# The opening of a transformer block: order of loads, normalisation and first projections

## Chip, cores and metric

One core of a Trainium2 chip. The metric is the device time of one execution in microseconds (us), median of several runs.

## What is computed

One pre-norm block over 2048 tokens of width 576: attention with 32 query heads of 18 columns that share one key and one value head, then a bilinear feed-forward part of width 4608.

```
S, D, H, Dh, F = 2048, 576, 32, 18, 4608
n  = layernorm(x)
q  = n @ wq          (32 heads);   k = n @ wk;   v = n @ wv      (one head each)
o  = softmax(q k^T * Dh**-0.5) v
h  = x + o @ wo
n2 = layernorm(h)
out = h + ((n2 @ w_gate) * (n2 @ w_up)) @ w_down
```

The layer norm has no weights. The order of the tokens inside the softmax's sum doesn't matter, and each token's output depends on its own row and on all keys and values, so tokens may be permuted inside the kernel if the output is put back in the same order.

## The kernel before

Tokens are worked in four blocks of 512 (`TB`), each as four tiles of 128 rows. The kernel gives each engine its program by hand (`manual_schedule`): the order of the Python calls is the order on each engine and on SP, which issues all DMAs. Matrices that need full precision are split into a high part (a cast to `fp32r`) and a low part (the rest, a subtraction), and a product is three matmul passes: high by high, high by low, low by high. A projection of one block is 14 such passes over 512 columns (`passes`, line 1187).

`keys_values` (line 131) is the opening. SP loads the tokens tile by tile, block 0, then the constants, the weights of keys and values (`wkr`) and of the first seven query heads (`wqr0`), then blocks 1 to 3, and last the other three query weights. Then:

- `stats` (line 166) takes mean and variance of a tile on VectorE; `scale` (171) takes the inverse root by Newton steps on VectorE (block 0) or POOL, with -mean x rstd always on POOL; `apply` (179) normalises a tile on ScalarE;
- `turn` (185) transposes a block on TensorE, 16 transposes into two large PSUM tiles `tr` and 8 for the last 128 rows into `trt`; `parts` (201) splits the result into the block's `XT`, the cast on ScalarE, the subtraction on VectorE (`split`, line 82; `split_tail`, line 91);
- `project` (212) makes queries of the last four heads, keys and values of one block (`psk`); `mean` and `keys` (217, 222) take the mean key of block 0 away and store the keys, in three parts, into `kT` by DMA; `values` (249) transposes values into `V`;
- `weights` (256) splits a query weight; `query` (262) makes 7 heads' queries of block 0, one matmul a step; `ready` (268) splits them, and `store_q` (363) takes their absolute values (`tq`) and stores the queries to memory;
- `bound` and `bounds` (240, 410) work out an upper bound of each query's scores (`psb`, `psg`), which `load_m` brings beside the queries from `load_q` (454, 460) as two more rows; with it the exponential needs no maximum.

`pair` (513) is one step of attention: two score matmuls over 128 keys and two heads each (`s`, two PSUM tiles of two banks in turn), and one exponential of 1024 columns on ScalarE (`P`, line 534). Two pairs and the `acc` matmuls (line 538) of earlier pairs are a `step`. The opening issues 14 pairs between its projections. A block and a group of four heads have 32 pairs, a block 256.

The main loop follows (line 1129): two pairs, then 1.9 units (`RATE`) of the generator `queries` for all blocks (380), which makes the queries of blocks 1 to 3, one unit being two half matmuls (line 389). For block 0 it only stores the last four heads, waits 7 units and makes the last bounds. Then `blocks` (1056) goes on with pairs up to the 256th (`steps`, line 994), beside output projections (`yo`, line 689) of block 0, and the feed-forward part, in which the attention of later blocks is mixed.

A tile of 128 tokens is 128 consecutive rows, one to a partition (lines 145, 877, 983).

Of the kernel before, what the change touches and what calls it, by code (L numbers as in the profile page):

```python
# [25 lines left out]
P = 128  # L26
# [28 lines left out]
class Block:  # L55
# [9 lines left out]

    def ps_s(self, name):
        return self.ps.tile([P, 2, TB], F32, tag="s", bufs=2, name=name)
# [34 lines left out]
    def rstd(self, var, name, eng=None, n=NQ):  # L102
# [6 lines left out]
        dve.tensor_scalar(v, var, 1e-5, None, ALU.add)  # L109
# [21 lines left out]
    def keys_values(self):  # L131
# [39 lines left out]
        def scale(lo, hi, eng):  # L171
            r = self.rstd(mv[:, lo:hi, 1], f"a{lo}", eng, hi - lo)
            n = self.lp.tile([P, hi - lo], F32, tag=f"n{hi - lo}", name=f"n{lo}")
            pool.tensor_tensor(n, mv[:, lo:hi, 0], r, ALU.mult)
            pool.tensor_scalar(n, n, -1.0, None, ALU.mult)
# [3 lines left out]
        def apply(b, lo=0, hi=NQ):  # L179
            for s in range(lo, hi):  # L180
                xh = xhs[s] = self.pp.tile([P, D], F32, tag="P", name=f"xh{b}_{s}") if b < 2 else xs[b][:, s, :]
                r, n = rs[NQ * b + s]
                act.activation(xh, xs[b][:, s, :], AF.Identity, bias=n, scale=r)

        def turn(b):

            tail = self.ps_m(f"trt{b}")
            for r in range(2):
                tr = self.ps_s(f"tr{b}_{r}").rearrange("p a (c q) -> p (a c) q", q=2 * P)
                for s in (2 * r, 2 * r + 1):  # L190
                    for c in range(4):
                        pe.transpose(tr[:, c, (s - 2 * r) * P:(s - 2 * r + 1) * P],
                                     xhs[s][:, c * P:(c + 1) * P], self.ident)
                trs.append((b, r, tr))
# [6 lines left out]
        def parts():  # L201

            while trs:
# [8 lines left out]
        def project(b):  # L212
            psk = psks[b] = (self.ps_a if b < 2 else self.ps_f)(f"psk{b}")
            for i, (w, m) in enumerate(passes(w_h, w_l, self.XT[b])):
                pe.matmul(psk[:6 * DH], w, m, start=(i == 0), stop=(i == 13))

# [32 lines left out]
        def values(lo, hi):  # L249
            psv = (self.ps_m if lo else self.ps_a)(f"psv{lo}").rearrange("p (t c) -> p t c", c=64)  # L250
# [5 lines left out]
        def weights(i, cast):  # L256

            w, r = cols[i], wqr[i]
            cast(self.wq_h[w], r)
            pool.tensor_tensor(self.wq_l[w], r, f32(self.wq_h[w]), ALU.subtract)  # L260

        def query(i):
            psq = psqs[i] = self.ps_f(f"psq0_{i}")
            for k, (w, m) in enumerate(passes(self.wq_h[cols[i]], self.wq_l[cols[i]], self.XT[0])):
# [3 lines left out]
        def ready(i, copy):  # L268
# [4 lines left out]
            self.store_q(0, 7 * i, 7, qs, 0 if i else 4)  # L273
            yield
# [11 lines left out]
        q0, q1, q2, q3 = (query(i) for i in range(4))  # L286
        act.copy(w_h, wkr)
        stats(0, 4)
        scale(0, 4, dve)
        apply(0)  # L290
        pool.tensor_tensor(w_l, wkr, f32(w_h), ALU.subtract)
        weights(0, act.copy)
        stats(4, 8)
        scale(4, 8, pool)
        turn(0)
        parts()
        weights(1, act.copy)
        weights(2, pool.tensor_copy)
        stats(8, 12)
        scale(8, 12, pool)  # L300
        project(0)
        apply(1)
        some(q0, 4)
        turn(1)
        some(q0, 10)
# [790 lines left out]
    def run(self):  # L1096
# [8 lines left out]
        with ExitStack() as st:  # L1105
# [38 lines left out]
            self.guard()  # L1144


RATE = 1.9
P_BUFS = 6
QS = 3

# [128 lines left out]
```

## Time and profile before

| | us |
|---|---|
| median of 3 runs (2287.66 to 2289.48) | 2287.97 |
| the profiled execution | 2291.63 |
| its span, first to last instruction | 2289.8 |
| TensorE busy / ScalarE / VectorE / POOL | 2263.5 / 1443.3 / 1175.7 / 681.6 |
| mean granted TensorE clock | 0.997 |

The span is what the profile's times count from; the rest of the execution's time lies around it. A busy TensorE isn't one at its peak: a matmul at half the clock is busy twice as long. The chain of work that ended last is followed back from the last instruction through whatever released each step. A row of the timeline gives start, length, engine, line, operation and tiles, how many instructions are merged in it, and in brackets how long the engine was idle before and who ended that.

### The profile page before, as it was taken

Reading aid. Unit: us, or ns where it says so; the run is one execution under the profiler, and the core shown is the slowest. Engines: PE = TensorE matmul, PEld = TensorE weight load, DVE = VectorE, ACT = ScalarE, POOL = GpSimd, SP = SyncE. Lnnn points to the kernel's source line nnn. Section 1 sums busy time; section 2 is a strip of 40 time slices with the busy share of each in tenths; the row PEclk is TensorE's granted clock in tenths of the full one; section 3 lists DMA queues with packets and bytes.
Section 4 is the critical chain, followed back from the end, with each engine's and each line's share of the span. In section 5 each row is a group of like instructions: output and inputs, shape, how many; then the busy total and the mean of one; then the engine's idle time right before and its main releaser. Section 6 shows DMA issues by size and latency. Waiting matters only on the chain.

```text
span 2289.8 us, 45889 instructions
## 1 busy us (share of the span) xinstructions
PE 2263.5 (99%) x18090; PEld 1609.9 (70%) x18090; DVE 1175.7 (51%) x2134; ACT 1443.3 (63%) x1884; POOL 681.6 (30%) x862
## 2 busy tenths in 40 slices
PE   7999999999999999999999999999999999999998
PEld 5333345777777677677777777777777788888887
DVE  6332246565656576344444455444444476566665
ACT  5899977667676765767677767667677623232332
POOL 4000002545545454222222222222122233333342
PEclk9999999999999999999999999999999999999999
DMA  4212224433334443633333344634233355655553
GB/s 157 77 62 84 81 83 128 150 136 134 126 126 151 146 158 118 215 116 125 102 117 120 125 128 125 193 117 125 94 122 122 113 180 172 213 171 171 176 187 112
DMA packets 129434, 306.76 MB, mean 134 GB/s; under 512 B 17809, under 2 KB 17937, under 8 KB 129209
## 3 DMA queue, kind: packets, MB, share of 16 engines
q1 hardware_dynamic: 129209, 303.73, 40.7%
q8 instruction: 145, 2.38, 0.4%
q14 instruction: 80, 0.66, 0.1%
HBM read 233.76 MB, written 55.67 MB: 126 GB/s over the span
## 4 chain that ended last, share of the span: by engine, by line
PE 96%; ACT 1%; DVE 1%; issue 1%; DMA 1%; POOL 0%; SPq 0%; DVEq 0%; ACTq 0%; POOLq 0%
PE pg L925 21%; PE acc L538 20%; PE y L885 17%; PE gu L925 13%; PE s L533 12%; PE pu L925 5%; PE yo L689 3%; PE psq L389 2%; PE y L843 1%; ACT P L534 0%; PE psq L265 0%; DMA X<-X 0%; PE ye L843 0%; DVE XT L85 0%; PE tx L758 0%
## 5 line engine op out<-in xcount | busy, mean ns | idle before, releaser
L534 ACT ACTIVATE P<-s 128x1024 f32<-128x1024 f32 x1024 | 1024.9, 1026 | 271.1 <-PE s L533 195.0
L925 PE MATMUL pu<-X,ws 64*128 64x512 f32 x2592 | 702.2, 389 | 0.1
L925 PE MATMUL pg<-X,ws 64*128 64x512 f32 x2592 | 702.0, 389 | 0.0
L925 PEld LDWEIGHTS pg<-X,ws 64*128 64x128 f32 x2592 | 479.3, 185 | 67.8 <-issue 1.2
L538 PE MATMUL acc<-P,V 128*32 128x512 f32 x4096 | 488.8, 599 | 0.0
L925 PEld LDWEIGHTS pu<-X,ws 64*128 64x128 f32 x2592 | 477.1, 185 | 14.0 <-DVE h L690 1.0
L533 PE MATMUL s<-q,kT 56*128 56x512 f32 x2048 | 454.7, 422 | 4.4 <-ACT P L534 2.3
L885 PEld LDWEIGHTS y<-wdo,room 128*128 128x128 f32 x2856 | 386.0, 188 | 46.9 <-issue 44.2
L885 PE MATMUL y<-wdo,room 128*128 128x288 f32 x2856 | 402.8, 300 | 0.0
L892 ACT COPY tmp<-y 128x288 f32<-128x288 f32 x408 | 162.6, 399 | 330.1 <-PE y L885 311.3
L533 PEld LDWEIGHTS s<-q,kT 56*128 56x128 f32 x2048 | 210.7, 184 | 193.9 <-ACT P L534 116.0
L925 PE MATMUL gu<-X,ws 64*128 64x512 f32 x2592 | 301.6, 389 | 0.0
L893 POOL TENSOR_TENSOR x<-x,tmp 128x288 f32<-128x288 f32 x204 | 158.9, 809 | 434.4 <-ACT tmp L892 433.6
L538 PEld LDWEIGHTS acc<-P,V 128*32 128x32 f32 x4096 | 114.0, 109 | 243.1 <-issue 234.6
L925 PEld LDWEIGHTS gu<-X,ws 64*128 64x128 f32 x2592 | 249.7, 184 | 46.1 <-issue 4.6
L84 POOL CAST ws<-wr 128x1152 fp32r<-128x1152 f32 x144 | 171.7, 1193 | 322.4 <-PE pu L925 186.6
L893 POOL TENSOR_TENSOR h<-h,tmp 128x288 f32<-128x288 f32 x204 | 158.9, 806 | 344.8 <-ACT tmp L892 344.4
L85 DVE TENSOR_TENSOR ws<-wr,ws 128x1152 fp32r<-128x1152 f32 x144 | 198.6, 1379 | 74.6 <-POOL ws L84 74.6
L959 DVE TENSOR_TENSOR hf<-pu,g 128x512 f32<-128x512 f32 x96 | 66.4, 691 | 262.5 <-ACT g L955 259.1
L888 DVE TENSOR_TENSOR x<-x,y 128x288 f32<-128x288 f32 x272 | 117.2, 453 | 144.8 <-PE y L885 144.8
L888 DVE TENSOR_TENSOR h<-h,y 128x288 f32<-128x288 f32 x272 | 118.0, 454 | 111.9 <-PE y L885 109.0
L85 DVE TENSOR_TENSOR room<-S,room 128x1024 fp32r<-128x1024 f32 x68 | 86.3, 1270 | 146.5 <-ACT room L84 146.5
(170 smaller groups left out, 1628.2 us busy)
## 6 DMA issues: line engine op xcount, KB each, us to landing
wdo<-wd_dram SPq DMA_DIRECT2D x369, 288.0 KB
wr<-in_wgu_dram SPq DMA_DIRECT2D x144, 576.0 KB
wd_dram<-wdo SPq DMA_DIRECT2D x123, 288.0 KB
q<-q_dram SPq DMA_DIRECT2D x64, 216.0 KB
raw<-in_wd_dram SPq DMA_DIRECT2D x36, 288.0 KB
q_dram<-qs SPq DMA_DIRECT2D x15, 504.0 KB
X<-X SPq DMA_DIRECT2D x24, 256.0 KB
x<-in_x_dram SPq DMA_DIRECT2D x16, 288.0 KB
```

Source lines behind the costliest of these rows:

```text
L84: (copy or self.cast)(hi, src)
L85: self.dve.tensor_tensor(lo, src, f32(hi), ALU.subtract)
L533: self.pe.matmul(s_[:, i], self.kT[o:o + 56, t * P:(t + 1) * P], q[o:o + 56, pr], start=True, stop=True)
L534: self.act.activation(p_, s_, AF.Exp, scale=SCALE)
L538: self.pe.matmul(acc[32 * j:32 * j + 32, :], self.V[:, t, :], Ps[j // 2][:, j % 2, :], start=(t == 0), stop=(t == NT - 1), skip_group_chec ...
L689: pe.matmul(y[:, :HD], m, k, start=(i == 0), stop=(i == len(ms) - 1))
L885: pe.matmul(y[:, :HD], m[:, t * P:(t + 1) * P], k, start=(first and j == 0), stop=(j == 2), skip_group_check=True)
L888: dve.tensor_tensor(hs, hs, y[:, :HD], ALU.add)
L892: act.copy(z, y[:, :HD])
L893: pool.tensor_tensor(hs, hs, z, ALU.add)
L925: pe.matmul(ps, w[o:o + 64, wk, c], X[o:o + 64, xk, c], start=(j == 0), stop=(j == 26))
L959: dve.tensor_tensor(hf, pu, g, ALU.mult)
```

## The change

- **Tokens.** A block's 512 tokens lie four consecutive rows to a partition: tile s holds rows 4p + s. Loads of whole blocks are one DMA; block 0 comes in three (tile 0, tile 1, tiles 2 and 3). The stores of the output follow.
- **Order of loads.** Block 0, constants, key and value weights, two query weights, block 1, two query weights, blocks 2 and 3. The raw query weights 1 to 3 lie in buffers that the output weights use later, not in those of the queries.
- **Statistics and normalisation.** The inverse root has one operation less; on VectorE -mean x rstd is one VectorE operation and not two on POOL. `apply` takes a list of tiles, and an engine: VectorE normalises tiles 0 and 1 of blocks 0, 1 and 3 and all of block 2, ScalarE the others.
- **TensorE.** 24 transposes of the identity into a scratch bank come first (`WARM`). A projection of block 0's queries or of keys runs all passes of high parts first (`highs_first`). The query tiles q0 and q1 come ahead of block 1's transposes, q2 ahead of block 1's keys; the first score pairs follow those keys.
- **Query weights.** High parts of weights 0 to 2 on ScalarE, of 3 on POOL, each apart from its low part; 0 and 1 ahead of the normalisation.
- **Storing.** `store_q` is a generator: first stores, then `tq`, then the rest. Block 0's last four heads and all its bounds are done in the opening; the main loop starts at block 1.
- **Later.** `steps` always takes two units of output projection.

```diff
+    def tokens(self, dram, b):
+        return dram[b * TB:(b + 1) * TB, :].rearrange("(p s) d -> p s d", s=NQ)
...
-        dve.tensor_scalar(v, var, 1e-5, None, ALU.add)
+        dve.tensor_scalar(v, var, 1e-5, -0.5, ALU.add, ALU.mult)
         dve.tensor_copy(t, v.bitcast(I32))
-        dve.tensor_scalar(yi, t, -0.5, 1597463007.0, ALU.mult, ALU.add)
-        dve.tensor_scalar(v, v, -0.5, None, ALU.mult)
+        dve.tensor_scalar(yi, t, -0.5, 519526879.0, ALU.mult, ALU.add)
...
-        wqr += [self.qb.tile([P, 5, 7 * DH], F32, tag="qs", bufs=QS, name=f"wqr{i}") for i in range(1, 4)]
-        for b in range(NB):
-            for s in range(NQ):
-                sp.dma_start(xs[b][:, s, :], self.x[b * TB + s * P: b * TB + (s + 1) * P, :])
-            if b == 0:
-                sp.dma_start(self.C, self.cst)
-                sp.dma_start(wkr, self.wkv)
-                sp.dma_start(wqr[0], self.wq[cols[0]])
-        for w, r in zip(cols[1:], wqr[1:]):
-            sp.dma_start(r, self.wq[w])
+        wqr += [self.w0.tile([P, 5, 7 * DH], F32, tag="wo_r", bufs=3, name=f"wqr{i}") for i in range(1, 4)]
+        for lo, hi in ((0, 1), (1, 2), (2, 4)):
+            sp.dma_start(xs[0][:, lo:hi], self.tokens(self.x, 0)[:, lo:hi])
+        sp.dma_start(self.C, self.cst)
+        sp.dma_start(wkr, self.wkv)
+        for i in range(2):
+            sp.dma_start(wqr[i], self.wq[cols[i]])
+        sp.dma_start(xs[1], self.tokens(self.x, 1))
+        for i in range(2, 4):
+            sp.dma_start(wqr[i], self.wq[cols[i]])
+        for b in range(2, NB):
+            sp.dma_start(xs[b], self.tokens(self.x, b))
...
+            else:
+                dve.scalar_tensor_tensor(n, mv[:, lo:hi, 0], -1.0, r, ALU.mult, ALU.mult)
...
+                if on is dve:
+                    dve.tensor_scalar(xh, xs[b][:, s, :], mv[:, NQ * b + s, 0:1], r, ALU.subtract, ALU.mult)
+                else:
+                    act.activation(xh, xs[b][:, s, :], AF.Identity, bias=n, scale=r)
...
-            for i, (w, m) in enumerate(passes(w_h, w_l, self.XT[b])):
+            for i, (w, m) in enumerate(highs_first(w_h, w_l, self.XT[b])):
...
+        warm = self.ps_a("warm")
+        for _ in range(WARM):
+            pe.transpose(warm[:, 0:P], self.ident, self.ident)
+        stats(0, 4)
+        highs(0, act.copy)
+        highs(1, act.copy)
+        scale(0, 4, dve)
+        apply(0, 0, 1, on=dve)
+        apply(0, 2, 3)
         act.copy(w_h, wkr)
+        turns(0)
+        stats(4, 6)
+        parts()
         pool.tensor_tensor(w_l, wkr, f32(w_h), ALU.subtract)
+        lows(0)
+        lows(1)
+        highs(2, act.copy)
+        lows(2)
+        stats(6, 8)
         scale(4, 8, pool)
+        drain(project(0))
         mean()
+        some(q0, 15)
+        stats(8, 9)
         k0 = keys(0)
+        some(k0)
+        stats(9, 10)
         g0 = bound(G0, 1)
+        some(q1, 3)
         some(g0)
         t0 = ready(0, act.copy)
+        some(t0, 2)
         some(g0)
         some(t0)
+        some(k0)
+        some(q1, 6)
+        self.bounds(0, act.copy, self.pp.tile([H, 2, TB], F32R, tag="P", name="m2_0"), G0)
+        apply(1, 0, 1, on=dve)
+        apply(1, 2, 3)
+        stats(10, 11)
+        some(q1, 6)
         q = self.qt[0, 0] = self.qp.tile([P, 2, TB], F32R, tag="q", name="q0_0")
         some(k0)
         self.load_q(q, 0, 0)
         self.load_m(q, 0, 0)
+        some(t0)
+        t1 = ready(1, act.copy)
+        some(t1)
+        stats(11, 12)
+        scale(8, 12, pool)
+        highs(3, pool.tensor_copy)
+        lows(3)
+        values(0, 4)
+        turns(1)
+        parts()
+        stats(12, 14)
+        scale(12, 14, pool)
+        some(q2, 15)
+        drain(project(1))
+        apply(2, 0, 1, 2, 3, on=dve)
         k1 = keys(1)
         some(k1, 2)
+        self.pair()
+        self.pair()
+        stats(14, 15)
+        t2 = ready(2, act.copy)
+        some(t2)
+        some(q3, 6)
+        turns(2)
         parts()
         some(k1)
+        some(q3, 4)
+        stats(15, 16)
+        scale(14, 16, dve)
+        step(q3, 0)
+        values(4, 8)
+        drain(project(2))
+        apply(3, 0, 1, on=dve)
+        apply(3, 2, 3)
+        drain(t1)
+        drain(t2)
+        turns(3)
         k2 = keys(2)
         some(k2, 2)
         parts()
         some(k2)
+        some(q3, 15)
+        drain(ready(3, dve.tensor_copy))
+        self.last_heads(0)
         step()
         step()
+        drain(project(3))
         k3 = keys(3)
         some(k3, 3)
+        step()
+        step()
         g0 = bound(self.G, 4)
         some(g0, 2)
         values(8, 16)
+        self.pair()
+        self.bounds(0)
+        self.pair()
+        self.flush(len(self.pend) - 1)
...
-        if b in (0, NB - 1):
-            yield 4 if b else 7
+        if b == NB - 1:
+            yield 4
             self.bounds(b)
...
-            self.outs(2 if len(self.yos) > 1 else 1)
+            self.outs(2)
...
-                        for b in range(NB):
+                        for b in range(1, NB):
                             yield from self.queries(b)
...
+WARM = 24
+def highs_first(W, Wl, XT):
+    p = passes(W, Wl, XT)
+    return p[0:12:3] + p[2:12:3] + p[1:12:3] + p[12:]
```

In the part from `warm` to `flush` the added lines stand in their new order; lines without a mark stand in both kernels, and the old order is in the listing above.

More of the change, by code (lines that the diff above doesn't have):

```diff
@@ L199, in turn, with turns, parts @@
             trs.append((b, None, tail))
-        def parts():
-            while trs:
+        def turns(b):
+            for r in range(2):
+                turn(b, r)
+            turn_tail(b)
+        def parts(n=3):
+            for _ in range(n):
                 b, r, tr = trs.pop(0)
@@ L333, in keys_values @@
         parts()
         some(k1)
-        some(q1, 3)
-        values(0, 8)
-        some(ready(1, dve.tensor_copy))
-        step(q2, 4)
-        step(q2, 3)
-        apply(3)
-        project(2)
-        turn(3)
+        some(q3, 4)
[9 more added lines that the diff above has]
+        turns(3)
         k2 = keys(2)
@@ L981, in load_x @@
         h = self.h[b] = self.hp.tile([P, NQ, D], F32, tag="h", name=f"h{b}")
[L982 to L983 removed]
+        self.sp.dma_start(h, self.tokens(self.x, b))
     def fill(self, time, keep=2):
```

107 lines of the change are left out of this document (38 added, 69 removed).

## The prediction

> **What bounds the kernel now.** I read the page first: the shares by engine and the chain that ended last.
>
> ```profile
> PE 2263.5 (99%) x18090; PEld 1609.9 (70%) x18090; DVE 1175.7 (51%) x2134; ACT 1443.3 (63%) x1884; POOL 681.6 (30%) x862
> PE 96%; ACT 1%; DVE 1%; issue 1%; DMA 1%; POOL 0%; SPq 0%; DVEq 0%; ACTq 0%; POOLq 0%
> ```
>
> TensorE carries 96% of the chain, so an opening that ends earlier moves everything behind it. What such a change can win is TensorE time that is empty or slow. I cut the opening into windows to find it; after the window and its length the columns are busy us (and instructions) of each engine, granted clock, DMA share and GB/s.
>
> ```profile
> 12.50:18.00 5.50, 5.43 (x25) 5.08 (x25) 3.75 (x10) 4.81 (x8) 2.62 (x6) 1.00 1.06 382
> 40.00:42.00 2.00, 0.18 (x4) 0.09 (x2) 1.94 (x4) 0.15 (x1) 1.50 (x8) 0.94 0.44 127
> 42.00:52.00 10.00, 10.00 (x28) 4.71 (x29) 2.52 (x4) 6.59 (x8) 1.92 (x2) 0.50 0.27 88
> 52.00:76.50 24.50, 23.97 (x142) 13.62 (x142) 10.20 (x16) 15.11 (x18) 0.00 (x0) 1.00 0.17 51
> 83.90:298.80 214.90, 214.67 (x1566) 80.36 (x1565) 66.54 (x118) 194.80 (x201) 2.10 (x3) 1.00 0.23 75
> ```
>
> Three losses show. TensorE starts at 12.57 us. It is empty for most of 40 to 42 us, and then has half the clock for 10 us, though "busy" all the while. From 84 us on it has no hole that an opening could fill. The timeline gives the steps that I will move (start, length, engine, line, operation):
>
> ```profile
> 11.38 0.24 POOL L175 TENSOR_SCALAR n<-n 128x4 f32<-128x4 f32 x1
> 11.65 3.15 ACT L183 ACTIVATE xh<-x,n,ya 128x576 f32<-128x576 f32 x4 [2.58 <-POOL n L175]
> 12.57 3.68 PE L192 MATMUL tr<-C,xh 128*128 128x128 f32 x16 [12.57 <-ACT xh L183]
> 16.04 1.92 PE L197 MATMUL trt<-C,xh 128*128 128x128 f32 x8
> 18.75 3.26 PE L215 MATMUL psk<-XT,wk 128*108 128x512 f32 x13 [0.56 <-DVE XT L85]
> 41.97 0.89 PE L533 MATMUL s<-q,kT 56*128 56x512 f32 x2 [1.82 <-DVE XT L94]
> 75.07 1.02 ACT L534 ACTIVATE P<-s 128x1024 f32<-128x1024 f32 x1 [1.24 <-PE s L533]
> ```
>
> So the milestones of the kernel before are: block 0 transposed at 17.96 (16.04 + 1.92), its keys projected at 22.0, first score matmul at 41.97, and the exponential at 75.07, the 14th, done at 76.1. Both kernels issue 14 score pairs before the main loop, so I compare at that milestone and then ask what the loop keeps.
>
> **The change part by part.** Prices come from these rows:
>
> ```profile
> 3.76 0.82 DVE L99 BATCH_NORM_STATS2 bsa<-x 128x6 f32<-128x288 f32 x2 [3.76 <-DMA x<-in_x_dram]
> 4.62 0.21 DVE L100 BATCH_NORM_AGGREGATE mv<-bsa 128x2 f32<-128x12 f32 x1
> 6.57 0.82 DVE L99 BATCH_NORM_STATS2 bsa<-x 128x6 f32<-128x288 f32 x2 [0.81 <-DMA x<-in_x_dram]
> L192 PEldq EVENT_SEMAPHORE  x5: 51/51/51, 7.7 to 52.0; - x5
> ...
> 8.43 0.64 ACT L287 CAST wk<-wkr 128x540 fp32r<-128x540 f32 x1 [6.42 <-DMA wkr<-in_wkv_dram]
> 8.59 0.17 DVE L109 TENSOR_SCALAR va<-mv 128x4 f32<-128x4 f32 x1
> 10.78 0.16 DVE L121 SCALAR_TENSOR_TENSOR ya<-ta,ya 128x4 f32<-128x4 f32 x1
> 14.70 0.70 ACT L259 CAST wq_h<-wqr 128x630 fp32r<-128x630 f32 x1
> 17.00 0.23 POOL L109 TENSOR_SCALAR va<-mv 128x4 f32<-128x4 f32 x1
> 18.73 0.69 DVE L94 TENSOR_TENSOR XT<-trt,XT 64x512 fp32r<-64x512 f32 x1
> 21.20 0.20 POOL L119 TENSOR_TENSOR ya<-ta,ya 128x4 f32<-128x4 f32 x1
> 358.84 2.05 DVE L738 TENSOR_SCALAR xh<-x,mvb,yb 128x576 f32<-128x576 f32 x4
> 25.64 1.90 ACT L84 CAST XT<-tr 128x1024 fp32r<-128x1024 f32 x2
> 26.67 2.36 DVE L85 TENSOR_TENSOR XT<-tr,XT 128x1024 fp32r<-128x1024 f32 x2 [0.75 <-ACT XT L84]
> 25.71 1.04 PE L197 MATMUL trt<-C,xh 128*128 128x128 f32 x8
> 33.08 3.38 PE L215 MATMUL psk<-XT,wk 128*108 128x512 f32 x14
> 61.51 3.77 ACT L534 ACTIVATE P<-s 128x1024 f32<-128x1024 f32 x4 [0.40 <-PE s L533]
> ```
>
> *To the last transpose of block 0.* Token loads keep their bytes. The third and fourth tile now come as one transfer, so their statistics (2 x 0.93 us) start between 6.57 (nothing lost) and about 7.5 (where the fourth was used before); I take 7.5, the landing of a pair being that of its last row: statistics end at 9.4. The inverse root was 13 small VectorE operations, 8.59 to 10.94, 0.18 each; one goes (the -0.5 joins the first), and the -mean x rstd that POOL did until 11.62 becomes one more: 13 x 0.18 = 2.35, done at 11.8. Then VectorE normalises two tiles (2.05/4 = 0.51 each) while ScalarE does two at 3.15/4 = 0.79: last at 13.5 against 14.80. The 24 warm-up transposes need the constants, for which TensorE's transpose line stops waiting at 7.7 here (the first of its five semaphore events); at the slow rate (1.92/8 = 0.24) they cost 5.8 and end at 13.5 at worst, ahead of nothing that is ready much sooner: price 0 to 0.6, taken as 0 since the warm rate (1.04/8 = 0.13) will come in the middle of them. The tail transposes then cost 1.04 and not 1.92: all 24 are done at about 15.3, **2.6 earlier**.
>
> *To block 0's keys.* Before, ScalarE's query-weight cast at 14.7 stood ahead of the casts of the transposed tokens; now two such casts run before the tokens are normalised, while ScalarE waits anyway. They are free if both weights land by about 11; the weight loads moved ahead of block 1 make that plausible (0.3 MB each at the 380 GB/s of the window row, behind keys that landed by 8.4); if late by a microsecond, that microsecond is paid. ScalarE then casts the key weights (0.64, until 14.2), the two halves (0.95 each, until 16.2) and the tail (16.8). VectorE has statistics of two tiles (until 15.1), the two low parts (1.18 each, 17.65), the tail 0.69 (18.35). TensorE, doing all high passes first, starts at 16.3 and is done when the 18.35 tail lets the last two through: 19.6 against 22.0, **2.4 earlier**. The reordering costs no matmul: 14 stay 14.
>
> *To the first score.* One query tile more stands ahead of it: q0 (3.4), q1 (3.4) with the two bound matmuls (0.8) and their waits end at 27.2. Block 1 is then late: POOL starts its inverse root at 20.2, after statistics, and takes 4.7 (17.00 to 21.7 before), then VectorE must first finish the bound's parts (27.2), so its tiles come at 28.3: TensorE idles about 1.1. Then transposes 2.1, q2 3.4, block 1's keys 3.4: 37.2 against 41.97, **4.8 earlier**. The first score also needs the queries and bounds back from memory. Before, these rows stood between:
>
> ```profile
> 34.59 1.15 SPq L423 DMA_DIRECT2D m_dram<-m  x1
> 38.16 0.53 SPq L463 DMA_DIRECT2D q<-m_dram  x2
> ```
>
> From 34.59 to the score at 41.97 are 7.4 us at most for that round trip; the store moves to about 27.3, so data is there by 34.7, 2.5 us ahead. On SP only loads of tokens and weights stand before it, all issued by 20. Gone with this: the hole at 40 to 42 us, and, I expect, the slow clock behind it. What is late next is VectorE, which now has ten of sixteen tiles to normalise (0.51 each, 5.1 us) and ScalarE ten fewer (7.9 us).
>
> *To the 14th exponential.* After the first score the old kernel did 29 us of TensorE work in 34.1. The new one has q3 (3.4), transposes of two blocks (5.1), their keys (6.8), six steps at 1.9 (11.4; two pairs at the 3.77/4 = 0.94 of ScalarE, the slower side of a step), the last pair, values and bounds (about 4): 31. I add 1.3 for two places where score banks come free only after VectorE's low part: after the q3 passes, and ahead of the pair behind block 3's transposes. 37.2 + 32.3 = **69.5 against 76.1: 6.6 earlier**.
>
> *Beyond.* The old loop held block 0's last bounds:
>
> ```profile
> 82.73 1.28 PE psg L416 x5
> 302.58 0.98 PE yo L689 x6
> 347.70 0.61 PE yo L689 x3
> 0.00:342.00 342.00, 248.24 (x256) 0.99 0.28 90
> ```
>
> (The first three are of the chain; the last counts the exponentials up to 342 us: 256.)
>
> The bounds now run in the opening, where I counted it: 1.3 back at most. The loop also loses an allowance of 7 units of waiting, 7/1.9 = 3.7 steps without query work; those steps turn up again before pair 256, without query work as before: 0. Always taking two output units per step spares the left-over after the steps (0.6 of TensorE) and makes some steps longer by 0.49: nothing to 0.6 gained. Loads and stores of four rows a partition keep their bytes; stores keep rows of 2304 B: 0. Against these I set 2 us for some thirty hand-overs between engines in my timetable that I gave 0.1 each or none. Total: 6.6 + 1.3 + 0.1 - 2.0 = **6.0 us**.
>
> The profiled execution took 2291.63 us (span 2289.8, 1.8 around it), 3.7 over the median of the runs, 2287.97. Profiled, I expect 2285.6; with the same gap, 2282.0.
>
> **One rule of the skill against the change.** The row of the 13 key matmuls gives 3.26/13 = 0.25 each at 18.75, where ahead of it stood only 24 transposes and one matmul; the transposes themselves ran at 0.24 at 16.04 and at 0.13 at 25.71. So transposes have here brought the clock up. The Trainium skill, TensorE: Matmul & The Clock Gate, Part 4: PE-mode transpose, says that the full clock doesn't engage for transposes, because they don't count as activity in the same way; by that the warm-up is idle work. The trace disagrees, so far as one start can show. As a mechanism here: block 0's 24 transposes at 0.24 end 2.6 later, and some 3.4 us of key matmuls run at half speed, 1.7 more; 6.0 - 4.3 leaves 1.7, time 2286.3. I give it a share of the second rival.
>
> **The rivals.**
> 1. *Well filled.* My two stalls and the 2 us of hand-overs don't appear, and block 1's normalisation is ready in time (1.1): 6.0 + 1.3 + 2.0 + 1.1 = 10.4, time 2277.5. For it: VectorE is busy only 10.2 of 24.5 us in the window from 52. Against: the order of the new opening makes TensorE wait at each block for VectorE. Chance 0.2.
> 2. *The clock is not won.* The new hole (about 1.6 us around 53 to 55 us) halves the clock as the 1.8 us did here, or the warm-up fails, or the timed runs never had the 10 slow microseconds (their median is 3.7 below the profiled run). A slow stretch is worth about 4.5: seven query matmuls, the first scores and values and half of a key projection at double length. Gain 1.5 to 2.3, time about 2286. Chance 0.25.
> 3. *VectorE becomes the bound: slower.* The last two rows are the same operation, its first beside a POOL subtraction, its second with POOL idle (the first row is that of all statistics, min/median/max in ns):
>
> ```profile
> L99 DVE BATCH_NORM_STATS2 bsa<-x x32: 405/443/462, 3.8 to 35.8; 128x6 f32<-128x288 f32 x32
> 43.44 1.11 DVE L368 SCALAR_TENSOR_TENSOR tq<-qs 126x512 fp32r<-126x512 f32 x1
> 61.22 0.68 DVE L368 SCALAR_TENSOR_TENSOR tq<-qs 126x512 fp32r<-126x512 f32 x1
> ```
>
> That is 0.43 per operation which meets POOL. Between 13 and 39 us the new VectorE queue has some 40 operations over 0.4 us, nearly all on the way to a TensorE step, and POOL works there for about 20 us. If 26 of them pay, 26 x 0.43 = 11.2: 5.2 slower than before, 2293.2; it decides from 14 such meetings on (6.0/0.43). Against: the statistics ran beside POOL's small operations for much of 19 to 25 us, and none of the 32 took over 0.46. Chance 0.1. (The Trainium skill, SBUF — State Buffer, Who interferes with whom, calls it an exclusive lock on the port pair that both share; the pair of rows fits that.)
>
> **How the numbers follow.** Forecast 2282.0, chance 0.45, by itself 2279.5 to 2284.5. This kernel's runs tell about 0.2%, 4.6 us, from no change: faster is below 2283.4, slower above 2292.5. The forecast's case is faster for 0.38 and within for 0.07; rival 1 is faster (0.2), rival 2 within (0.25). Rival 3 is slower at its price, within with a few meetings less: 0.08 and 0.02. Together faster 0.58, same 0.34, slower 0.08. The range must take in rival 1 and rival 2 with its bounds, and leaves out most of rival 3: 2275.5 to 2289.0.
>
> **What would show it.** Right: the first transposes of tokens at 12.5 to 13.5 us and eight tail transposes in 1.04; keys of block 0 done near 19.6; first score near 37; no window of clock 0.50 between 20 and 70 us; the 14th exponential done near 69.5; the 256th some 6 us ahead of the 342 of before. Wrong: a clock of 0.50 again, a first score after 40 us whose releaser is a DMA, statistics or low parts over their durations beside POOL, or an advance at the 14th exponential that is gone at the 256th.

## The result, and the profile after

The changed kernel takes 2292.7 us (median of 16 runs, 2290.42 to 2297.66), the kernel before 2288.69 (16 runs, 2286.94 to 2292.33). The ratio is 1.0019, with a 95% interval of 1.0012 to 1.0026: some 4 us slower, where 6 us faster were forecast. The profiled execution of the changed kernel took 2295.69 us (span 2293.8), 4.1 more than that of the kernel before.

The opening first. This is the changed kernel's timeline, TensorE and then the other engines (start, length, engine, line, operation):

```profile
8.47 5.12 PE L307 MATMUL warm<-C 128*128 128x128 f32 x24 [8.47 <-DMA C<-in_cst_dram]
13.43 1.91 PE L201 MATMUL tr<-C,xh 128*128 128x128 f32 x16
15.17 1.04 PE L210 MATMUL trt<-C,xh 128*128 128x128 f32 x8
16.67 3.58 PE L233 MATMUL psk<-XT,wk 128*108 128x512 f32 x14 [0.47 <-ACT XT L88]
38.02 0.74 PE L591 MATMUL s<-q,kT 56*128 56x512 f32 x4
...
8.04 0.82 DVE L103 BATCH_NORM_STATS2 bsa<-x 128x6 f32<-128x288 f32 x2 [2.42 <-DMA x<-in_x_dram]
12.53 1.06 DVE L192 TENSOR_SCALAR xh<-x,mv,ya 128x576 f32<-128x576 f32 x2
12.64 1.63 ACT L194 ACTIVATE xh<-x,n,ya 128x576 f32<-128x576 f32 x2 [0.56 <-DVE n L183]
72.87 1.02 ACT L592 ACTIVATE P<-s 128x1024 f32<-128x1024 f32 x1 [1.98 <-PE s L591]
```

It follows the forecast closely up to the first score: tail transposes in 1.04, block 0 transposed at 16.2 (15.17 + 1.04; forecast 15.3), its keys done at 20.2 (19.6), first score 38.02 (37.2). The 14th exponential ends at 73.9, where 69.5 was forecast. Windows of the same execution (TensorE, its weight loads, VectorE, ScalarE, POOL busy; then clock, DMA share, GB/s) show what lies between:

```profile
40.00:50.00 10.00, 9.13 (x58) 6.09 (x57) 9.22 (x27) 6.17 (x9) 3.47 (x15) 1.00 0.31 104
50.00:60.00 10.00, 8.80 (x59) 5.12 (x58) 9.73 (x16) 8.93 (x11) 0.00 (x0) 1.00 0.16 47
67.80:74.60 6.80, 6.55 (x28) 2.36 (x27) 2.67 (x6) 2.10 (x3) 0.00 (x0) 0.50 0.09 24
```

VectorE is nearly full for 20 us while TensorE has holes, and then this execution too has a stretch of half clock, 6.8 us long. Still, the 14th exponential is 2.2 us ahead of the 76.1 of before. By 342 us it has done 258 exponentials where the kernel before has 256, and its 256th ends at 340.4 against 341.95: 1.5 us ahead, where some 6 were forecast (window, length, ScalarE's busy time and number of exponentials, clock, DMA share, GB/s):

```profile
0.00:342.00 342.00, 249.00 (x258) 0.99 0.28 91
```

So the lead is smaller than forecast, but the loss isn't here. To find it, I cut both executions at the first feed-forward matmul (`pg`) and at the first one of the part that no longer has attention beside it (`gu`). These windows are of the kernel before:

```profile
0.00:366.00 366.00, 347.51 (x2359) 152.14 (x2359) 151.25 (x316) 297.43 (x320) 32.57 (x82) 0.99 0.27 86
366.00:1826.00 1460.00, 1458.78 (x12019) 1056.91 (x12019) 740.10 (x1315) 1007.88 (x1295) 483.11 (x586) 1.00 0.42 134
1826.00:2289.80 463.80, 457.17 (x3718) 400.87 (x3714) 284.31 (x505) 137.99 (x270) 165.92 (x194) 1.00 0.51 171
```

And these of the changed one:

```profile
0.00:363.30 363.30, 348.14 (x2383) 154.21 (x2384) 159.52 (x337) 290.69 (x313) 32.64 (x76) 0.99 0.27 87
363.30:1830.20 1466.90, 1465.80 (x12021) 1050.03 (x12019) 737.86 (x1313) 1008.32 (x1295) 482.12 (x586) 1.00 0.41 133
1830.20:2293.80 463.60, 456.79 (x3718) 403.81 (x3714) 283.98 (x504) 137.78 (x270) 166.11 (x194) 1.00 0.51 171
```

The first part is 2.7 us shorter, the last one equal. **The middle part, where the diff changes no instruction of TensorE, is 6.9 us longer**, at full clock, with the same work (12019 and 12021 matmuls, a few records can be missing) and TensorE as full as before: 1.2 and 1.1 us of it are empty. (What the diff changes there is which rows the loads and stores of tokens take.) Nothing waits longer; the matmuls themselves take longer. The page has them among its groups (busy us, mean ns of one), before and after; `pg` and `pu` are the gate and the up half of the feed-forward part, `acc` belongs to the attention beside them:

```profile
L925 PE MATMUL pu<-X,ws 64*128 64x512 f32 x2592 | 702.2, 389 | 0.1
L925 PE MATMUL pg<-X,ws 64*128 64x512 f32 x2592 | 702.0, 389 | 0.0
L538 PE MATMUL acc<-P,V 128*32 128x512 f32 x4096 | 488.8, 599 | 0.0
```
```profile
L984 PE MATMUL pu<-X,ws 64*128 64x512 f32 x2592 | 707.0, 391 | 0.1
L984 PE MATMUL pg<-X,ws 64*128 64x512 f32 x2592 | 707.0, 391 | 0.0
L596 PE MATMUL acc<-P,V 128*32 128x512 f32 x4096 | 488.8, 599 | 0.0
```

`pu` and `pg` alone have 10 us more of busy time (overlaps counted twice), `acc` has none. The question for the runs was why matmuls of the same shapes in the same order are slower hundreds of us after the opening. The order of TensorE's instructions from the first `pg` on is the same in both kernels, so what differs, beside the rows of loads and stores, is *where the tiles lie*: the change moves two things by side effect. In PSUM, the scratch tile `warm` is the first to be taken of the large tiles, so the banks of the others rotate: `acc` comes from bank 5 into bank 0 and the one-bank tiles from 0 into 5. In SBUF, a second group of small tiles (`n2`, two tokens' tiles at a time, beside `n4`) takes 2 x 32 bytes of each partition, and the three buffers of output weights grow from 576 to 630 columns to hold raw query weights (2304 to 2528 bytes, 3 x 224 = 672). Residuals, queries and exponentials so move up by 64 bytes, and the feed-forward tokens `X` and weights `ws` by 736.

The measure in all that follows is the **stretch**: first start of `gu` less first start of `pg`. Each is read from the rows of these tiles (min/median/max ns of one, then first and last start): of the kernel before

```profile
L925 PE MATMUL pg<-X,ws x2592: 383/388/501, 366.2 to 1822.1; 64*128 64x512 f32 x200
L925 PE MATMUL gu<-X,ws x2592: 383/386/497, 1826.2 to 2276.0; 64*128 64x512 f32 x200
```

and of the changed one

```profile
L984 PE MATMUL pg<-X,ws x2592: 383/392/502, 363.3 to 1826.1; 64*128 64x512 f32 x200
L984 PE MATMUL gu<-X,ws x2592: 383/386/502, 1830.2 to 2279.9; 64*128 64x512 f32 x200
```

1826.2 - 366.2 = 1460.0, and 1830.2 - 363.3 = 1466.9; the median `pg` goes from 388 to 392 ns, `gu` stays at 386. The stretch begins after the opening, and the granted clock in it is 1.00 in every trace here. Six executions with the tiles of the main part at the SBUF places of before lie between 1460.0 and 1460.8, three with those of the changed kernel between 1465.9 and 1466.9, so a single execution tells some 6 us.

### The profile page after: what moved, and what is told of

It reads as the page before. It is cut to its first block, busy times and chain, and to the rows that moved or that the text cites. A ratio compares the mean times of both kernels' runs of the same rounds, so it can differ in the third digit from the quotient of the medians.

```text
span 2293.8 us, 45921 instructions
## 1 busy us (share of the span) xinstructions
PE 2270.7 (99%) x18114; PEld 1608.0 (70%) x18114; DVE 1181.4 (52%) x2152; ACT 1436.8 (63%) x1877; POOL 680.9 (30%) x856
## 4 chain that ended last, share of the span: by engine, by line
```

## The experiments

**Banks or bytes.** The theory: tiles' places in SBUF. The rival: those in PSUM. Four kernels cross them, all timed in 11 runs beside 33 of the kernel before (2288.59). `new_old_banks` is the changed kernel with the warm-up in a one-bank tile, so that the banks are those of before:

```diff
-        warm = self.ps_a("warm")
+        warm = self.ps_m("warm")
```

> The changed kernel with its scratch bank for the warm-up taken from the other one-bank group, so that every PSUM tile lies where it lay before (sums of attention in bank 5, not 0; output tiles of one bank in 0, not 5); nothing else differs. Measure: from the first gate matmul of the feed-forward part beside attention to the first one without attention, 1459.9 us before and 1466.8 after. Theory PSUM: the loss comes from the exchanged banks, so the stretch returns to 1460 and the kernel is some 7 us faster than the changed one, 2285 to 2286 beside 2288.7. Theory SBUF (tiles lie 64 to 736 bytes further on): stretch stays at 1467, time 2292 to 2293. Theory third cause (order of tokens, one load a block): also 1467.

`new_old_sbuf` is the changed kernel with every tile of the main part at its old place: raw query weights lie in the (still empty) buffer of keys and values, output weights have their 576 columns, and there is one group of small tiles.

```diff
-        wqr += [self.w0.tile([P, 5, 7 * DH], F32, tag="wo_r", bufs=3, name=f"wqr{i}") for i in range(1, 4)]
+        wqr += [self.kvq.rearrange("p a b -> p (a b)")[:, i * 630:(i + 1) * 630].rearrange("p (c m) -> p c m", c=5) for i in range(3)]
...
-            n = self.lp.tile([P, hi - lo], F32, tag=f"n{hi - lo}", name=f"n{lo}")
+            n = self.lp.tile([P, 4], F32, tag="n4", name=f"n{lo}")[:, 0:hi - lo]
...
-        w = self.w0.tile([P, 5, 7 * DH], F32, tag="wo_r", bufs=3, name=f"wo_r{c}")
-        r = self.wo_r0[c] = w.rearrange("p a b -> p (a b)")[:, 0:D]
+        r = self.wo_r0[c] = self.w0.tile([P, D], F32, tag="wo_r", bufs=3, name=f"wo_r{c}")
```

> The changed kernel with the raw query weights 1 to 3 in the still empty buffer of keys and values, and the small -mean x rstd tiles in one group, so that the tiles of the feed-forward part lie at the SBUF addresses of before (X at 102816 and not 103552 of a partition, exponentials from 40192 and not 40256); banks stay those of the changed kernel. Theory SBUF: stretch returns to 1460, time 2285 to 2286. Theory PSUM: stretch 1467, time 2292 to 2293. Third cause: 1467. If each place has half of it: about 1463 here and with the old banks.

`old_new_banks` is the kernel before with the new banks, and `old_new_sbuf` the kernel before with the new places:

```diff
+        first = self.ps_a("first")
+        dve.memset(first[:, 0:1], 0.0)
```

> The kernel before with one bank taken first, by a small memset on VectorE, so that banks 0 and 5 are exchanged as in the changed kernel, and nothing else. Theory PSUM: the stretch grows from 1459.9 to 1467, time 2295 to 2296 against 2288.7 (ratio 1.003). Theory SBUF and third cause: 1460, time within 1 us of before (the memset costs 0.1 on VectorE while it waits for tokens).

```diff
-            n = self.lp.tile([P, hi - lo], F32, tag=f"n{hi - lo}", name=f"n{lo}")
+            n = self.lp.tile([P, 12], F32, tag="n4", name=f"n{lo}")[:, 0:hi - lo]
...
-        r = self.wo_r0[c] = self.w0.tile([P, D], F32, tag="wo_r", bufs=3, name=f"wo_r{c}")
+        r = self.wo_r0[c] = self.w0.tile([P, 630], F32, tag="wo_r", bufs=3, name=f"wo_r{c}")[:, 0:D]
```

> The kernel before with three buffers of 576 columns made 630 wide and a small tile made wider, so that the tiles of the feed-forward part lie at the SBUF addresses of the changed kernel; no instruction differs. Theory SBUF: stretch 1467, time 2295 to 2296. Theory PSUM and third cause: stretch 1460, time within 1 us of before.

| code | banks | places in SBUF | stretch | median us | ratio to before (95%) |
|---|---|---|---|---|---|
| before | old | old | 1460.0 | 2288.59 | |
| before | new | old | 1460.7 | 2290.63 | 1.0001 (0.9992 to 1.001) |
| before | old | new | 1465.9 | 2294.63 | 1.0024 (1.0015 to 1.0033) |
| changed | new | new | 1466.9 | 2292.7 | 1.0019 (1.0012 to 1.0026) |
| changed | old | new | 1466.5 | 2292.38 | 1.0017 (1.0008 to 1.0027) |
| changed | new | old | 1460.8 | 2286.78 | 0.9991 (0.9982 to 1.0) |

(The ratios aren't the quotients of these medians: for the second line that would be 1.0009. The fourth line has its own runs of before, as above. In the second, six of 11 executions have a mean granted clock of 0.998 or below, of which more further down; the median of the other five is 2287.96.) The two rows that decide are the kernel before with the new places, slow,

```profile
L925 PE MATMUL pg<-X,ws x2592: 383/392/501, 365.0 to 1826.8; 64*128 64x512 f32 x200
L925 PE MATMUL gu<-X,ws x2592: 383/386/502, 1830.9 to 2280.7; 64*128 64x512 f32 x200
```

and the changed kernel with the old places, fast:

```profile
L983 PE MATMUL pg<-X,ws x2592: 383/388/498, 360.1 to 1816.7; 64*128 64x512 f32 x200
L983 PE MATMUL gu<-X,ws x2592: 383/386/498, 1820.9 to 2271.2; 64*128 64x512 f32 x200
```

The stretch and the median of `pg` follow the places, whatever the code and the banks. That the places of tiles in SBUF cost the 6 us is shown, from both sides; PSUM banks have no part in it that these runs can see. The order of tokens, loads and stores is out as well: the fast `new_old_sbuf` has the new one, the slow `old_new_sbuf` the old one.

**Which bytes.** All the next ones are the kernel before with tiles shifted by unused bytes, one execution each; the kernel before took 2288.24 beside the first four. `old_sbuf_all64` moves everything behind the small tiles by 64 (their `n4` of 4 becomes 16 columns), `old_sbuf_all128` by 128 (24 columns), `old_sbuf_w672` moves only `X` and the weights, by 672 (output weights of 630 columns, as above), `old_sbuf_w96` the same by 96 (584 columns).

> The kernel before with a small tile 64 bytes wider, so that every tile behind it (h, q, exponentials, X, weights) lies 64 bytes further on, the distance between them kept. Known: all of the changed kernel's places give a stretch (first gate matmul beside attention to the first without) of 1465.9 to 1466.8, those of before 1459.9 to 1460.8. Theory exponentials (P and q moved by 64): 1466. Theory weights and X (their places moved by 672 more): 1460. Theory alignment of X to 64 (before 32 over a multiple, changed 0 over): stays 32 over, 1460.

> The kernel before with the three buffers of the output weights 630 and not 576 columns wide: X, the weights and what lies behind them 672 bytes further on, h, q and the exponentials as before. Theory exponentials: 1460. Theory weights and X: 1466. Theory alignment of X to 64: it now lies on a multiple, 1466.

> The kernel before with the same three buffers 584 columns wide: X and weights 96 bytes further on, X on a multiple of 256. Theory alignment to 64: 1466, though they moved by 96 alone. Theory of a distance (672 or 736 from the exponentials matters as such): 1460. If the alignment to 128 or 256 counts the other way, under 1460.

> The kernel before with everything behind the small tile 128 bytes further on: exponentials on a multiple of 128 again, X 32 over a multiple of 64 still. Theory alignment of X to 64: 1460. Theory alignment of exponentials to 128: 1460, where the kernel with 64 gives 1466. Neither: something else.

Then, to move tiles against each other: `old_sbuf_rest96` makes `X` 96 bytes longer, so that `X` stays and the weights behind it move by 96. `old_sbuf_P64` moves residuals, queries and exponentials by 64, with `X` at its old place. `old_sbuf_Ponly` leaves the queries too, and moves the exponentials alone.

```diff
-        X = self.X = self.wp.tile([P, 2, 9, TB], F32R, tag="X", bufs=1, name=f"X{b}")
+        X = self.X = self.wp.tile([P, 18 * TB + 24], F32R, tag="X", bufs=1, name=f"X{b}")[:, 0:18 * TB].rearrange("p (k c q) -> p k c q", k=2, c=9)
```

> The kernel before with the tile X 96 bytes longer: X stays at 102816, and the weights (raw, split and those from memory) and all behind them lie 96 bytes further on. With X moved too, the stretch beside attention was 1467.3 against 1459.9. Theory that X's place decides: 1460. Theory that the weights' place decides: 1467. Theory of the distance between X and weights: neither of these, since it never changed so far.

```diff
-        nmean, kab, kabq = (p0.tile([P, 1], F32, name=n) for n in ("nmean", "kab", "kabq"))
+        three = p0.tile([P, 3], F32, name="three")
+        nmean, kab, kabq = (three[:, i:i + 1] for i in range(3))
...
-            n = self.lp.tile([P, hi - lo], F32, tag=f"n{hi - lo}", name=f"n{lo}")
+            n = self.lp.tile([P, 16], F32, tag="n4", name=f"n{lo}")[:, 0:hi - lo]
```

> The kernel before with residuals, queries and exponentials 64 bytes further on and X, weights and all behind them in place (three one-column tiles put together make up for the wider small tile). Everything moved by 64 gave 1471.1. Theory that the place of X or weights decides: 1460. Theory that the place of the exponentials that ScalarE writes and TensorE reads decides as well: up to 1471.

```diff
+        pad = self.qp.tile([P, 8], F32, tag="pad", name="pad")
+        pool.memset(pad, 0.0)
...
-        nmean, kab, kabq = (p0.tile([P, 1], F32, name=n) for n in ("nmean", "kab", "kabq"))
+        three = p0.tile([P, 3], F32, name="three")
+        nmean, kab, kabq = (three[:, i:i + 1] for i in range(3))
```

> The kernel before with only the exponentials (and two small tiles of the opening and the normalised heads ob behind them) 64 bytes further on; queries, residuals, X and weights stay. With queries and residuals moved too the stretch beside attention was 1466.0. Theory that the place of the exponentials against X and the weights decides: 1466. Theory that the queries' place against the keys decides: 1460.

| moved, bytes | residuals, queries | exponentials | X | weights | stretch | us, one execution |
|---|---|---|---|---|---|---|
| before | 0 | 0 | 0 | 0 | 1460.0 | 2291.63 |
| all64 | 64 | 64 | 64 | 64 | 1471.1 | 2302.93 |
| all128 | 128 | 128 | 128 | 128 | 1467.8 | 2295.81 |
| w672 | 0 | 0 | 672 | 672 | 1461.2 | 2291.35 |
| w96 | 0 | 0 | 96 | 96 | 1467.3 | 2293.9 |
| rest96 | 0 | 0 | 0 | 96 | 1467.0 | 2307.33 |
| P64 | 64 | 64 | 0 | 0 | 1466.0 | 2293.2 |
| Ponly | 0 | 64 | 0 | 0 | 1460.2 | 2290.16 |

(The times are of one execution each, some with a stretch of half clock in the opening and some without; the stretch is the measure.) Two of my rules fell here. That a place of `X` on a multiple of 64 bytes is slow, and one 32 bytes over it fast, doesn't hold: `old_sbuf_w672` puts `X` on a multiple and is fast, while all64, all128 and P64 leave it 32 over, as before, and are slow. That the exponentials lie badly doesn't hold either: alone, they cost nothing. By the last two lines it takes the residuals or the queries, moved by 64 together with the exponentials, to make the stretch 6 us longer; by `w96` it can also be `X` and the weights, and by 672 these move at almost no cost. In P64 the matmuls that slow down read only tiles that haven't moved, `X` and the weights:

```profile
L926 PE MATMUL pg<-X,ws x2592: 383/390/502, 361.7 to 1823.5; 64*128 64x512 f32 x200
```

So a matmul's speed here doesn't hang on the places of its own operands alone. The kernel that moves everything together by 64 is the slowest of the attention's stretches. The one that parts weights from `X` differs in kind: it also slows the part without attention,

```profile
L925 PE MATMUL pg<-X,ws x2592: 385/390/498, 366.0 to 1828.8; 64*128 64x512 f32 x200
L925 PE MATMUL gu<-X,ws x2592: 386/393/507, 1833.0 to 2291.7; 64*128 64x512 f32 x200
```

where `gu` goes from 386 to 393 ns, while every other kernel has 386, and its window from the first `gu` on

```profile
1833.00:2305.40 472.40, 465.84 (x3718) 397.80 (x3714) 283.96 (x504) 137.83 (x270) 166.21 (x194) 1.00 0.51 168
```

is 472.4 us long against 463.8, on the same 3718 matmuls. In `old_sbuf_w96` the weights lie at the very same bytes, but `X` has moved along, and `gu` is at 386: so in this part the place of the weights counts *relative to* `X`, as far as one execution of each shows. For the part with attention it isn't settled which places collide: these runs don't tell whether it is relative places again, and of which pair, and I have no rule that would have told a good place from a bad one.

**How much each of the two side effects costs.** `new_small_tile` is the changed kernel with one group of small tiles (the pair of lines with `n4` in the diff of `new_old_sbuf`), the output weights still wide; `new_all_places` has old banks and old places together.

> The changed kernel with the small tiles of -mean x rstd in one group of buffers and not two, nothing else: h, queries and exponentials lie where they lay before, X and the weights 672 bytes further on (and not 736). The kernel before with X and weights moved by 672 alone had a stretch of 1461.2. Theory that the 64 bytes of the second group of small tiles are the loss: 1461 and 2287, as with all old addresses. Theory that the weights' 672 count in the changed kernel: 1466, 2292.

> The changed kernel with SBUF addresses and PSUM banks of before, as the version to beat both: stretch 1460 to 1461, time 2286 to 2287, 1.5 to 2.5 under the kernel before. If banks and addresses had an effect together that neither showed alone, it would come out under 2285 or over 2288.

Taking back the small tiles' 64 bytes alone brings the stretch from 1466.9 to 1462.4, 4.5 of the 6.1 that `new_old_sbuf` wins (1460.8). The two effects don't add up, though: on the code of before, 64 bytes alone cost 11.1, 672 alone 1.2, and both together 5.9. In whole time `new_small_tile` takes 2287.97, ratio 0.9994 (0.9985 to 1.0003). `new_all_places` has 1460.7 and 2287.23, 0.9991 (0.9982 to 1.0), no different from old places alone. Both stand beside 21 runs of before (2290.26).

**The warm-up and the outputs.** On `new_old_sbuf`, `new_warm1` has one warm-up transpose in place of 24, and `new_old_outs` takes the number of output units by the old rule. Both were timed in 10 runs, beside 19 of before (2290.07).

```diff
-WARM = 24
+WARM = 1
```

> The changed kernel at the old SBUF addresses (2286.8 us) with one warm-up transpose and not 24. If transposes bring the clock up, block 0's 24 transposes run at 0.21 to 0.24 each again, and the first score, at about 39.6 with 24, comes 1.5 to 3 us later; of the whole time 1 to 2 us are lost, 2288 to 2289. If they don't count as activity: no difference, 2286.8.

```diff
-            self.outs(2)
+            self.outs(2 if len(self.yos) > 1 else 1)
```

> The changed kernel at the old SBUF addresses with the old rule for the output units of a step (two only while another group waits). From the 256th exponential to the first gate matmul the kernel before takes 24.3 us and the changed one 22.9. Theory that no left-over output units are the reason: 24.3 again, and 1.4 us lost of the whole, 2288.2. Rival (the order of the opening gives it): 22.9 and 2286.8.

The opening of `new_warm1`:

```profile
12.77 3.67 PE L201 MATMUL tr<-C,xh 128*128 128x128 f32 x16 [4.19 <-DVE xh L192]
16.24 1.91 PE L210 MATMUL trt<-C,xh 128*128 128x128 f32 x8
17.80 3.45 PE L233 MATMUL psk<-XT,wk 128*108 128x512 f32 x13
```

Without the warm-up a tail transpose takes 0.24 and not 0.13, block 0 is transposed at 18.15 in place of 16.40 (`new_old_sbuf`), and the first exponential ends at 41.40 in place of 40.05. So the warm-up works. In the whole time it isn't seen: 2287.41, ratio 0.9986 (0.9977 to 0.9996), against 0.9991 (0.9982 to 1.0) with it. The outputs aren't either: 2286.7, 0.9984 (0.9975 to 0.9994). In the traces they are. These three rows end with the 256th exponential, in `old_new_banks`, `new_old_sbuf` and `new_old_outs`:

```profile
335.28 1.94 ACT L536 ACTIVATE P<-s 128x1024 f32<-128x1024 f32 x2 [0.32 <-PE s L535]
335.20 1.94 ACT L592 ACTIVATE P<-s 128x1024 f32<-128x1024 f32 x2
335.14 1.94 ACT L592 ACTIVATE P<-s 128x1024 f32<-128x1024 f32 x2 [0.32 <-PE s L591]
```

| opening, at full clock | 14th exponential ends | 256th ends | first `pg` starts | 256th to `pg` |
|---|---|---|---|---|
| old (`old_new_banks`) | 71.16 | 337.22 | 361.49 | 24.3 |
| new (`new_old_sbuf`) | 71.86 | 337.14 | 360.05 | 22.9 |
| new, old rule for the outputs (`new_old_outs`) | 72.41 | 337.08 | 360.98 | 23.9 |

From the 256th exponential to the first `pg` all ten traces of the code before take 24.3, the six of the changed code with two units 22.9, and the one with the old rule 23.9. So 1.0 of these 1.4 us is the output units; where the other 0.4 comes from isn't shown.

The kernel that beats both, changed code on the old places, thus gains 0.1% on the kernel before, at the edge of what these runs tell.

## Why the prediction was wrong, point by point

**The step that failed** is the last part of the sum, "Beyond": it carries the opening's gain to the end of the kernel, and what else moves, such as loads and stores of four rows a partition, it puts at 0. The prediction counted instructions, transfers and waits that move. For tiles that move in memory it had no term, and gave no reason for that; under "Order of loads" the change says that raw weights lie in other buffers, and this was read only as a question of who waits for whom. In its place stand **+6.1 us** (1466.9 - 1460.8, changed kernel; 1465.9 - 1460.7 = 5.2 with the code of before), accrued hundreds of us behind the opening, where the diff changes no instruction of TensorE. This turns the sign.

**The mis-sized term** is "69.5 against 76.1: 6.6 earlier". My side of it was nearly right. The 76.1 was not typical: it holds the half clock from 42 to 52 us, and that comes in some executions only. The same windows of `old_new_banks`, whose opening is the old one, show the same hole of VectorE's wait and no half clock:

```profile
40.00:42.00 2.00, 0.68 (x3) 0.47 (x4) 1.94 (x4) 0.06 (x1) 1.58 (x7) 1.00 0.23 60
42.00:52.00 10.00, 9.99 (x60) 6.77 (x61) 3.51 (x6) 9.39 (x12) 1.37 (x1) 1.00 0.29 92
```

Its 14th exponential ends at 71.16, 4.9 ahead of the profiled execution of before:

```profile
70.14 1.02 ACT L536 ACTIVATE P<-s 128x1024 f32<-128x1024 f32 x1 [1.24 <-PE s L535]
```

The new opening without a half clock, that of `new_old_sbuf`, has it at 71.86. That is 2.4 over the 69.5, of which the prediction had booked 2.0 apart for hand-overs. So, of two openings at full clock, the new one is 0.7 *later* at this milestone, though it was 2.9 ahead at the first exponential (40.05 against 42.97). In the loop, which no longer holds block 0's bounds, it makes 0.8 good (the forecast had 1.3 at most; no run shows apart that the bounds are the reason), and at the 256th it is level, 337.14 against 337.22. The other traces without a half clock say the same: the 256th ends at 336.8 to 337.6 with the old opening (four) and at 336.9 to 337.1 with the new (five). Only behind it comes the lead of 1.4 at the first `pg`, and 1.0 of that are the output units, for which the prediction gave 0 to 0.6 and took 0.1. So at full clock the new order of the opening by itself gains next to nothing. Forecast from an undisturbed old opening, the sum would have been 71.16 - 69.5 + 1.4 - 2.0 = 1.1, not 6.0; that this is near the 1.4 measured is in part luck, since the opening was 0.4 worse than booked, the loop gave 0.5 less back, and the part behind the 256th 1.3 more.

How often the half clock comes can be told from the mean granted clock: executions of 0.998 or below have it in the traces I have, those of 0.999 or above don't (the end of the kernel takes the rest). Of the 73 executions of the kernel before that stand beside the experiments, 28 are at or below 0.998, and take 1.6 to 2.3 us more than the others of their group in the median (2290.58 against 2288.32, 2290.92 against 2288.64, 2290.82 against 2289.2). The profiled one had 0.997 and the long form, 10.2 us; the median of before, 2287.97, is the time of one without. This is what rival 2 named: its clause "the timed runs never had the 10 slow microseconds", with the 3.7 us between the profiled run and the median as evidence, was nearest, and had a quarter of the chances. Its gain of 1.5 to 2.3 also agrees with the changed code on the old places (2286.78 against 2288.59, 1.8), but 1.0 of that is the output units, which it doesn't price. I argued from the profiled execution and took the gain off the median, which has no such stretch to win.

**Sum.** Opening and output units at full clock, about -2 (medians at 0.999 or above: 2286.62 for `new_old_sbuf`, 2288.32 beside it); places +6; together +4, and 2292.7 - 2288.69 = 4.0.

**What held.** The warm-up at a price of 0, tail transposes in 1.04, keys, first score within 0.8. The 1.3 us set aside for score banks that come free only after VectorE's low part: they show in `new_old_sbuf` as 1.8, in three waits.

```profile
PE s L591 <- DVE XT L89: 1.8, 3, 0.6
PE s L591 <- ACT P L592: 1.1, 2, 0.6
```

The statistics of the third and fourth tile start at 8.04 (taken 7.5), and the weights' casts that I called free (10.28 and 11.37 in the trace) are.

**The transposes and the clock.** The prediction set the row against the Trainium skill, TensorE: Matmul & The Clock Gate, Part 4: PE-mode transpose, by which the full clock doesn't engage for transposes. The runs bear the row out: after 24 transposes and nothing else, the token transposes take 0.12 to 0.13 each, and after one they take 0.23 to 0.24. The granted clock of the profile reads 1.00 in both cases, so it is the durations alone that show the change of pace. The 2286.3 that the prediction worked out for the opposite case plays no part in the miss.

**Rival 3** gave 2293.2, and the time agrees with it to 0.5 us. The mechanism doesn't. It put 11 us of loss into the opening; at full clock the opening is level with the old one by the 256th exponential, VectorE's low parts of 512 columns took 0.64 to 0.70 in `new_old_sbuf`, and the changed code on old places isn't slower than before. VectorE did become what limits 40 to 60 us (9.2 and 9.7 of 10), as the forecast's own "late next" says, without that price. A time that agrees is no proof of its mechanism.

## What to carry to other kernels

A kernel that keeps TensorE busy for 99% of its time can be slowed by a buffer that grows: when a change adds or resizes a tile, ask which tiles of the main loop move by it, and pin them (a spare tile, an order of pools) before reading what the code itself does. Cut both traces at milestones that both have, and look at the parts the diff doesn't touch first. And before you sell a slow stretch of a profile as the gain, ask whether the median execution has it: a profiled time above the median is a warning. Then count the milestones on to the main part: here a lead of 2.9 us at the first exponential was gone at the 256th.

## What the runs showed of the hardware that was not expected

- **Places of tiles in SBUF set how fast TensorE streams**, with nothing waiting in the records: `pg` 386, 388, 390, 392 or 393 ns in the median by kernel, the stretch from 1460.0 to 1471.1 us, `gu` 386 or 393. (The two don't go strictly together: the 386 is of `old_sbuf_w672`, with 1461.2 us.) The Trainium skill, SBUF — State Buffer, Who interferes with whom, has one rule, that only the port pair of VectorE and GpSimd causes contention, and says that TensorE never waits on anyone; the runs here disagree, or show a cost that the rule doesn't cover. What the collision is, no run here shows.
- **The half clock comes in some executions and not in others, at the same place.** In the ten traces with the opening of before, TensorE has a hole of 1.6 to 2.2 us ahead of the first score, which starts at 41.3 to 42.0; it is followed by 10.2 us of half clock in three, by 6.8 in three and by none in four. The length of the hole doesn't decide: 1.62 (`old_sbuf_w672`) has it and 1.84 (`old_sbuf_all128`) hasn't. The changed kernel's trace has it at 67.8, that of `new_warm1` from about 69; 2 of the changed kernel's 16 runs are at 0.998 or below.
- **Transposes alone bring TensorE to full pace.** The 24 of the warm-up take 0.21 us each on average (5.12 in all), the token transposes behind them 0.12 to 0.13; behind a single one (`new_warm1`) they take 0.23 to 0.24.
